# From a weave over two batches to a pipeline over three: linear attention, transposes and attention experts on one Trainium2 core

## The chip, the core and the metric

The kernel runs on one core of a Trainium2 chip. TensorE does matmuls and transposes, VectorE and ScalarE move PSUM to SBUF and do elementwise work, GpSimd does elementwise work on SBUF, and SyncE issues the DMAs. The metric is the device time of one execution in microseconds.

## The reference, cut to what matters

For each of 8 batches a linear attention over 8 heads (576 tokens, 64 dimensions) gives x, and x goes through 4 causal attention experts of which each token uses 2.

```python
kv  = einsum('bhsd,bhse->bhde', k, v)            # linear attention
out = einsum('bhsd,bhde->bhse', q, kv)
x   = out / sqrt(mean(out*out, -1) + 1e-6) * g_norm   # (B, 576, 512)
logits = x @ w_gate                              # top 2 of 4 experts, softmax of the two
for e in range(4):
    q, k, v = x @ wq[e], x @ wk[e], x @ wv[e]    # 512 -> 64
    a = softmax(causal(q @ k.T / 8))
    y += weight[e] * (a @ v @ wo[e])             # where e is one of the token's two
```

## The kernel before

Tokens are handled in five blocks (four of 128 and one of 64). `stage1(b)` is the linear attention of a batch: `p_kv` sums k and v over tokens (L179), `kv_copy` takes it out of PSUM (L187 on VectorE into `kvx`, L188 on ScalarE into `kv2`), `q_block` transposes q (L200), `p_kt` and `p_kg` fold the gate's weights in (L216, L224), and `p_out` (L243) multiplies q by the result. `o_sb` (L250, VectorE), `sq` (L254, ScalarE) and `ms` (L260, VectorE) give the mean squares of a block. Then a chain of small operations on VectorE makes the inverse root by Newton's method: `half` (L271), a first `y` (L273), four passes of `u`, `w`, `y` (L279 to L281). With the last `y`, VectorE makes the gate's logits (L284, L290) and GpSimd the normalized tokens `x_tok`, one tile a block (L296). TensorE transposes these (`p_x`, L307), and ScalarE copies them into `xT`.

`stage2(b)` is the experts: the gate on VectorE (`max`, `sh`, `mk`, `gt`, `gate`, L322 to L341, with an exponential `ex` on ScalarE), the values `p_v` (L347), then for two pairs of experts the projections `p_proj` (L365, cast by ScalarE into `qTp` and `kT`, L376), the scores `p_sc` (L393) with their exponentials into `PT` (ScalarE, L403) and the causal mask (GpSimd, L408), the products `p_O` (L445) with their scaling `osc` (VectorE, L460 to L465), and the transposes `p_OT` (L477). `final(b)` multiplies by `wo` (`p_y`, L501), copies (`y`, L506) and issues the output's DMA; it runs inside the experts of the next batch.

The stages are generators that yield estimated costs. `weave` runs `stage2(b)` and takes pieces of `stage1(b + 1)` so that the latter's `p_out` ends at 72% of the former; the tail of `stage1` (chain, `x_tok`, `p_x`) comes after that. Program order sets priorities; a scheduler may move instructions that are ready. PSUM has two pools: three buffers of two banks ("big": `p_out`, `p_proj`, `p_sc`, `p_O`) and two of one bank ("small": `p_q`, `p_kv`, `p_kt`, `p_kg`, `p_x`, `p_v`, `p_OT`, `p_y`). All DMAs are issued from SyncE's queue in order; the loads of batch b + 2 are issued when step b starts, into one of two sets of buffers.

Of the kernel before, what the change touches and what calls it, by code (L numbers as in the profile page):

```python
# [18 lines left out]
def kernel(  # L19
# [170 lines left out]

    def stage1(b, res):
        qb, kb, vb = loads[b]
# [123 lines left out]

    def stage2(b, res, prev_y):
        xT = res["xT"]
# [25 lines left out]
        for i, (t0, nt) in enumerate(blocks):
            p_v = small([P, E * Hd], "p_v")
            for c in range(NCH):
                nc.tensor.matmul(  # L347
                    p_v[:nt, :],
                    lhsT=xT[:, c, t0 : t0 + nt],
                    rhs=w_r["v"][:, c, :, :].rearrange("p e f -> p (e f)"),  # L350
                    start=(c == 0),
                    stop=(c == NCH - 1),
                )
            nc.vector.tensor_copy(  # L354
                out=vx[:nt, i, :, 0:Hd], in_=p_v[:nt].rearrange("p (e f) -> p e f", e=E)
            )
            yield 0.47

        def proj(pr):
            out_t = []  # L360
            for nm in ("q", "k"):
# [18 lines left out]
                yield 1.0  # L380
            res["qk", pr] = out_t

        def scores(pr):
# [47 lines left out]

        def pv(pr):
            PT = res["PT", pr]
            p_O = big("p_O")
            inv = moe.tile([P, NB, 2], FP32, tag="inv", name="inv")
            osc = moe.tile([P, NB, 2, Hd], BF16, tag="osc", name="osc")
            groups = ((0, (0, 1, 2)), (1, (3, 4)))
            for bank, qcs in groups:
                for n, qc in enumerate(qcs):
                    s0, nq = blocks[qc]  # L440
                    for el in range(2):
                        for kb in range(qc + 1):
# [67 lines left out]

    W1, W2 = 14.0, 14.3
    OUT_END = 11.6 / W1

    def target(a):
        if a < 0.92:
            return min(a / 0.72, 1.0) * OUT_END
        return 1.0

    def weave(main, side):
        a = s = 0.0  # L520
        live = side is not None
        for c in main:
            a += c / W2
            while live and s < target(a):
                try:
                    s += next(side) / W1
                except StopIteration:
                    live = False
        if live:
            for _ in side:  # L530
                pass

    res = {}
    for _ in stage1(0, res):
        pass
# [40 lines left out]
```

## Time and profile before

| | |
|---|---|
| Time, median of 3 runs | 362.43 us (361.71 to 363.38) |
| The profiled execution | 362.53 us, span 360.7 us |
| Mean granted TensorE clock | 0.837 |
| TensorE busy | 291.8 us (81% of the span) |
| VectorE, ScalarE, GpSimd busy | 52%, 42%, 22% |
| HBM traffic | 40.30 MB, mean 112 GB/s |

The profile lists busy time, not useful time: a matmul at granted clock 0.5 (1.2 GHz) is busy longer than one at 1.0 (2.4 GHz). The span runs from the first to the last instruction; the time of an execution also holds what lies around it.

### The profile page before, as it was taken

To read this page: it belongs to the slowest core of one execution; us is meant where nothing else is said; L and a number is where in the kernel's file an instruction comes from. 1 tells how busy PE (TensorE), PEld (TensorE's weight loads), DVE (VectorE), ACT (ScalarE), POOL (GpSimd) and SP (SyncE) were. 2 spreads that over 40 slices of the span, in tenths; PEclk is the share of its full clock that TensorE was granted. 3 is DMA by queue.
4 is the path that set the end of the run, shared out by engine and by line. 5 is a ranking of instruction groups with operands and counts; after the bars stand their busy time and mean duration, and the time that the engine had idled before them with its cause. 6 is when DMAs were issued, how large, how long until landed. Compare 5 with 4: busy or idle time off the path is not lost.

```text
span 360.7 us, 6721 instructions
## 1 busy us (share of the span) xinstructions
PE 291.8 (81%) x2616; PEld 234.8 (65%) x2624; DVE 188.2 (52%) x561; ACT 153.0 (42%) x273; POOL 80.4 (22%) x148
## 2 busy tenths in 40 slices
PE   2782898849994999949995899949996799949883
PEld 2581687638863788638964698638874598728551
DVE  0259654772458444781558444781458534783040
ACT  0202345432581336622572326722663326713833
POOL 8000602150220502150220502141210502132220
PEclk9997599977997599956998599966998589965966
DMA  7968999901737066600872056700002000300213
GB/s 218 214 167 222 241 266 263 207 16 45 220 89 176 2 207 135 185 0 13 250 177 87 2 159 164 195 11 2 2 37 93 2 2 0 133 1 2 88 45 132
DMA packets 75280, 40.30 MB, mean 112 GB/s; under 512 B 54000, under 2 KB 70384, under 8 KB 75248
## 3 DMA queue, kind: packets, MB, share of 16 engines
q1 hardware_dynamic: 75248, 39.86, 42.6%
q8 instruction: 21, 0.34, 0.4%
q14 instruction: 11, 0.09, 0.1%
HBM read 30.42 MB, written 9.44 MB: 110 GB/s over the span
## 4 chain that ended last, share of the span: by engine, by line
PE 56%; issue 22%; ACT 9%; POOL 5%; DVE 4%; DMA 1%; SPq 1%; DVEq 0%; ACTq 0%; POOLq 0%
PE p_proj L365 11%; PE p_x L307 10%; PE p_v L347 7%; PE p_kv L179 7%; PE p_q L200 5%; PE p_out L243 5%; ACT PT L403 4%; POOL x_tok L296 4%; PE p_sc L393 4%; PE p_kg L224 2%; PE p_y L501 2%; DVE o_sb L250 2%; DMA v_b<-in_v_dram 1%; POOL PT L408 1%; ACT y L506 1%
## 5 line engine op out<-in xcount | busy, mean ns | idle before, releaser
L307 PE MATMUL p_x<-ident_f,x_tok 128*128 128x128 f32 (+1 forms) x160 | 39.2, 411 | 39.2 <-POOL x_tok L296 38.1
L408 POOL TENSOR_SCALAR_AFFINE_SELECT PT<-PT 128x256 bf16<-128x256 bf16 (+1 forms) x80 | 29.9, 383 | 167.8 <-ACT PT L403 167.0
L296 POOL TENSOR_TENSOR x_tok<-o_sb,y 128x512 f32<-128x512 f32 (+1 forms) x40 | 42.1, 1083 | 96.7 <-DVE y L281 96.7
L403 ACT ACTIVATE PT<-p_sc 128x576 bf16<-128x576 f32 (+3 forms) x80 | 53.5, 712 | 17.7 <-PE p_sc L393 17.6
L307 PEld LDWEIGHTS p_x<-ident_f,x_tok 128*128 128x128 f32 (+1 forms) x160 | 26.9, 216 | 48.5 <-POOL x_tok L296 45.3
L243 PE MATMUL p_out<-kvx,qT 128*128 128x136 f32 (+1 forms) x320 | 45.8, 291 | 1.6 <-ACT PT L403 0.6
L243 PEld LDWEIGHTS p_out<-kvx,qT 128*128 128x128 f32 (+1 forms) x320 | 38.9, 182 | 6.3 <-ACT PT L403 3.3
L205 DVE COPY qT<-p_q 128x512 f32<-128x512 f32 (+1 forms) x40 | 24.8, 637 | 27.7 <-PE p_q L200 27.7
L354 DVE CAST vext<-p_v 128x256 bf16<-128x256 f32 (+1 forms) x40 | 17.0, 425 | 39.5 <-PE p_v L347 39.1
L254 ACT ACTIVATE sq<-p_out 128x512 f32<-128x512 f32 (+1 forms) x40 | 23.8, 595 | 27.8 <-DVE o_sb L250 19.2
L250 DVE COPY o_sb<-p_out 128x544 f32<-128x544 f32 (+1 forms) x40 | 28.8, 720 | 12.9 <-PE p_out L243 10.6
L260 DVE TENSOR_REDUCE ms<-sq 128x8 f32<-128x520 f32 (+1 forms) x40 | 27.3, 684 | 12.7 <-ACT sq L254 12.7
L445 PE MATMUL p_O<-vext,PT 128*128 128x65 bf16 (+2 forms) x480 | 29.1, 200 | 4.9 <-DVE osc L465 4.2
L179 PE MATMUL p_kv<-v_b,k_b 128*64 128x64 f32 x512 | 28.1, 275 | 6.0 <-DMA v_b<-in_v_dram 5.9
L445 PEld LDWEIGHTS <-PT 128*128 128x128 bf16 (+2 forms) x480 | 23.2, 103 | 13.8 <-issue 9.7
L179 PEld LDWEIGHTS p_kv<-v_b,k_b 128*64 128x64 f32 x512 | 25.2, 187 | 8.0 <-DMA k_b<-in_k_dram 4.5
L347 PE MATMUL p_v<-wv_r,xT 128*128 128x256 f32 (+1 forms) x160 | 30.4, 329 | 0.0
L312 ACT CAST xT<-p_x 128x512 fp32r<-128x512 f32 (+1 forms) x40 | 21.7, 543 | 18.0 <-PE p_x L307 17.9
L393 PE MATMUL p_sc<-qTp,kT 64*128 64x288 f32 (+2 forms) x192 | 25.0, 338 | 2.3 <-ACT PT L403 1.5
L347 PEld LDWEIGHTS p_v<-wv_r,xT 128*128 128x128 f32 (+1 forms) x160 | 25.0, 215 | 1.8
L365 PE MATMUL p_proj<-xT,wq_r 128*128 128x288 f32 x128 | 25.7, 321 | 0.3 <-ACT PT L403 0.3
L501 PE MATMUL p_y<-wo_b,OT 128*128 128x512 bf16 (+1 forms) x72 | 23.4, 409 | 1.8 <-ACT OT L482 1.4
(67 smaller groups left out, 370.5 us busy)
## 6 DMA issues: line engine op xcount, KB each, us to landing
q_b<-in_q_dram SPq DMA_DIRECT2D x32, 256.0 KB, 4.7
out_dram<-y SPq DMA_DIRECT2D x32, 256.0 KB, 2.0
k_b<-in_k_dram SPq DMA_DIRECT2D x7, 1024.0 KB, 5.8
v_b<-in_v_dram SPq DMA_DIRECT2D x7, 1024.0 KB, 8.6
k_b<-in_k_dram SPq DMA_DIRECT2D x4, 256.0 KB, 4.2
v_b<-in_v_dram SPq DMA_DIRECT2D x4, 256.0 KB, 4.5
k_rem<-in_k_dram SPq DMA_DIRECT2D x8, 128.0 KB, 8.5
v_rem<-in_v_dram SPq DMA_DIRECT2D x8, 128.0 KB, 7.5
```

Source lines behind the costliest of these rows:

```text
L179: nc.tensor.matmul(p_kv[hh * Dh : (hh + 1) * Dh, c, :], lhsT=lk, rhs=rv, start=(j == 0), stop=(j == NF), skip_group_check=True,)
L243: nc.tensor.matmul(p_o[:nt, c // 2, (c % 2) * 2 * GW : (c % 2 + 1) * 2 * GW], lhsT=qT[:, c, t0 : t0 + nt], rhs=kvb[:, c, :, :].rearrange(" ...
L250: nc.vector.tensor_copy(out=ob[:nt, i].rearrange("p (k h) g -> p k (h g)", k=2), in_=p_o[:nt, :, 0 : 4 * GW])
L296: nc.gpsimd.tensor_tensor(out=xt[:nt], in0=ob[:nt, i, :, 0:Dh], in1=y[:nt, i * H : (i + 1) * H].unsqueeze(2).to_broadcast([nt, H, Dh]), op ...
L307: nc.tensor.transpose(p_x[:, c, :nt], xts[i][:nt, 2 * c : 2 * c + 2, :].rearrange("p h d -> p (h d)"), ident_f[:nt, :nt],)
L347: nc.tensor.matmul(p_v[:nt, :], lhsT=xT[:, c, t0 : t0 + nt], rhs=w_r["v"][:, c, :, :].rearrange("p e f -> p (e f)"), start=(c == 0), stop= ...
L365: nc.tensor.matmul(p_p[:, s, 0:HALF], lhsT=w_r[nm][:, c, 2 * pr : 2 * pr + 2, :].rearrange("p e f -> p (e f)"), rhs=xT[:, c, s * HALF : (s ...
L393: nc.tensor.matmul(p_s[:, el, o : o + hi - lo], lhsT=kTp[pb, kb * P : (kb + 1) * P], rhs=qTp[pb, lo:hi], start=True, stop=True,)
L403: nc.scalar.activation(PT[:, :, d0 : d0 + o], p_s[:, :, 0:o], ACTF.Exp, scale=scale)
L408: nc.gpsimd.affine_select(out=d, in_=d, compare_op=AluOpType.is_ge, fill=0.0, base=0, pattern=[[0, 2], [1, w]], channel_multiplier=-1,)
L445: nc.tensor.matmul(p_O[:nq, bank, (2 * n + el) * (Hd + 1) : (2 * n + el + 1) * (Hd + 1)], lhsT=PT[:nk, el, col : col + nq], rhs=vx[:nk, kb ...
L501: nc.tensor.matmul(p_y[:nq, :], lhsT=OT[:, pr, s0 : s0 + nq], rhs=wo_b[:, pr, :], start=(pr == 0), stop=(pr == EP - 1),)
```

## The change

`stage1` is split. `stage_a(b)` holds the linear attention up to `x_tok`, now with three Newton passes instead of four (and the factor subtracted the other way round, `reverse0=True`, so that no sign alternates). `stage_x(b)` holds the transposes `p_x` and the copies into `xT`. `stage2` becomes `stage_s`: `p_v` is a generator of its own, and a string of keys sets the order in which the pieces of one batch's experts are taken. `merge` takes pieces from up to three streams, each spread over a given part of the step: the experts of b over all of it, the transposes of b + 1 from 0.05 to 0.4, the linear attention of b + 2 from 0.1 on. A prologue does the attention of batch 0, and then the transposes of batch 0 and the attention of batch 1 side by side. Loads are issued one batch further ahead (b + 3 when step b starts).

```diff
-    def stage1(b, res):
+    def stage_a(b, res):
...
-        for it in range(4):
+        for it in range(3):
...
             xts.append(xt)
-        yield 0.0
+        res["x_tok"] = xts
+
+
+    def stage_x(res):
+        xts = res["x_tok"]
+        xT = s1.tile([P, NCH, S], FP32R, tag="xT", name="xT")
         for i, (t0, nt) in enumerate(blocks):
             p_x = small([P, NCH, P], "p_x")
...
-    def stage2(b, res, prev_y):
+    def stage_s(b, res, prev_y):
...
-        yield from proj(0)
-        yield from scores(0)
-        yield from proj(1)
-        yield from scores(1)
-        if prev_y is not None:
-            yield from prev_y
-        yield from pv(0)
-        yield from o_t(0)
-        yield from pv(1)
-        yield from o_t(1)
-        res["OT"] = OT
-
+        st = {"V": v_proj(), "Q0": proj(0), "Q1": proj(1), "S0": scores(0), "S1": scores(1)}
+        st.update({"P0": pv(0), "P1": pv(1), "T0": o_t(0), "T1": o_t(1), "Y": prev_y})
+        order = (
+            "Q0 Q0 V V S0 V S0 V S0 V S0 Q1 S0 Q1 S1 Y S1 Y S1 P0 P0 P0 S1 P0 P0 S1 Y T0 Y Y P1 P1 P1 P1 P1 T1"
+        )
+        for key in order.split():
+            if st[key] is not None:
+                yield next(st[key])
...
+    def merge(*streams):
+        live = [[t0, t0, (t1 - t0) / cost, gen] for gen, cost, t0, t1 in streams if gen is not None]
+        while live:
+            x = min(live, key=lambda x: x[0])
+            try:
+                x[0] += next(x[3]) * x[2]
+            except StopIteration:
+                live.remove(x)
+
+    CA, CX, CS = 11.8, 2.25, 14.5
+    res = [dict() for _ in range(B)]
+    merge((stage_a(0, res[0]), CA, 0.0, 1.0))
+    loads[2] = load_qkv(2)
+    merge((stage_x(res[0]), CX, 0.3, 0.6), (stage_a(1, res[1]), CA, 0.0, 1.0))
     y_gen = None
     for b in range(B):
-        if b + 2 < B:
-            loads[b + 2] = load_qkv(b + 2)
-        nxt = {}
-        weave(stage2(b, res, y_gen), stage1(b + 1, nxt) if b + 1 < B else None)
-        y_gen = final(b, res["OT"])
-        res = nxt
+        if b + 3 < B:
+            loads[b + 3] = load_qkv(b + 3)
+        merge(
+            (stage_s(b, res[b], y_gen), CS, 0.0, 1.0),
+            (stage_x(res[b + 1]) if b + 1 < B else None, CX, 0.05, 0.4),
+            (stage_a(b + 2, res[b + 2]) if b + 2 < B else None, CA, 0.1, 1.0),
+        )
+        y_gen = final(b, res[b]["OT"])
```

How this moves instructions, at two places. First TensorE's queue at the seam of two steps (line, operation, out<-in, shape, count). Before, `p_x` follows directly on the last `p_OT` of the experts:

```order
L477 MATMUL p_OT<-ident_b,osc 128x64
L307 MATMUL p_x<-ident_f,x_tok 128x128 x12
...
L307 MATMUL p_x<-ident_f,x_tok 128x128 x4
L365 MATMUL p_proj<-xT,wq_r 128x288
L307 MATMUL p_x<-ident_f,x_tok 128x64 x4
L365 MATMUL p_proj<-xT,wk_r 128x288
L347 MATMUL p_v<-wv_r,xT 128x256 x4
L179 MATMUL p_kv<-v_b,k_b 64x64 x8
```

Now the last `p_out` of batch b + 2 is followed by the projections of the next step, the rest of `p_O` and `p_OT` (18 and 5, left out here but for one each), and its first scores; `p_x` of batch b + 2 comes after these, one block before `p_kv` of the batch after it:

```order
L242 MATMUL p_out<-kvx_110,qT 64x136 x4
L373 MATMUL p_proj<-xT,wq_r 128x288 x8
L373 MATMUL p_proj<-xT,wk_r 128x288 x3
...
L451 MATMUL p_O<-vext_116,PT 128x65
...
L484 MATMUL p_OT<-ident_b,osc 128x128
L373 MATMUL p_proj<-xT,wk_r 128x288 x5
...
L400 MATMUL p_sc<-qTp,kT_134 128x320 x2
L313 MATMUL p_x<-ident_f,x_tok 128x128 x4
L179 MATMUL p_kv<-v_b,k_b 64x64 x8
```

Between the last `p_out` and `p_x` there are now 16 projections and 8 score matmuls that stood behind `p_x` before.

Second VectorE's queue at the same seam. Before, the last `ms` stands behind `osc` of both groups of `p_O`, and the copy of `p_v` (`vext`) is the first thing after `gate`:

```order
L465 TENSOR_TENSOR osc<-p_O,inv 128x384
L465 TENSOR_TENSOR osc<-p_O,inv 128x128
L460 RECIPROCAL inv<-p_O 64x2
L260 TENSOR_REDUCE ms_118<-sq_124 64x8
...
L341 TENSOR_TENSOR gate<-gt,rden 128x20
L354 CAST vext_116<-p_v 128x4x64
L187 COPY kvx_96<-p_kv 64x4x64
```

Now the last `ms` stands ahead of the second group's `osc`, and behind `gate` come both copies of `p_kv`, then those of `p_v`:

```order
L472 TENSOR_TENSOR osc<-p_O,inv 128x384
L259 TENSOR_REDUCE ms_104<-sq_124 64x8
L270 TENSOR_SCALAR half<-ms_104 128x40
...
L472 TENSOR_TENSOR osc<-p_O,inv 128x128
...
L347 TENSOR_TENSOR gate<-gt,rden 128x20
L187 COPY kvx_110<-p_kv 64x4x64 x2
L362 CAST vext_116<-p_v 128x4x64 x4
```

`ms` of the last block moved past one group of `osc`, and `p_kv`'s copies past `p_v`'s.

## Rows read from the trace of the kernel before

**Rows 1.** The page: busy us, share of the span and count, by engine.

```profile
PE 291.8 (81%) x2616; PEld 234.8 (65%) x2624; DVE 188.2 (52%) x561; ACT 153.0 (42%) x273; POOL 80.4 (22%) x148
```

**Rows 2.** Chain that ended last, in time order: start us, us, what.

```profile
198.65 1.19 POOL x_tok L296
```

**Rows 3.** TensorE in order of time: start us, us, line, tiles, count, [idle before].

```profile
199.88 3.15 PE L307 MATMUL p_x<-ident_f,x_tok 128*128 128x128 f32 x12 [4.31 <-POOL x_tok L296]
...
207.06 1.12 PE L179 MATMUL p_kv<-v_b,k_b 128*64 128x64 f32 x16
...
209.23 0.63 PE L179 MATMUL p_kv<-v_b,k_b 128*64 128x64 f32 x16
...
230.98 1.14 PE L243 MATMUL p_out<-kvx,qT 128*64 128x136 f32 x8
...
240.88 3.15 PE L307 MATMUL p_x<-ident_f,x_tok 128*128 128x128 f32 x12 [4.30 <-POOL x_tok L296]
```

**Rows 4.** Windows of one period: length, busy by engine (count), clock share, DMA.

```profile
195.60:199.90 4.30, 0.02 (x1) 0.02 (x1) 3.90 (x24) 0.64 (x1) 1.25 (x2) 0.50 0.00 0
199.90:209.20 9.30, 9.12 (x71) 7.57 (x73) 3.11 (x7) 3.48 (x7) 3.96 (x4) 0.50 0.01 2
209.20:234.00 24.80, 24.55 (x242) 19.93 (x240) 13.67 (x28) 14.78 (x26) 3.73 (x10) 1.00 0.69 186
234.00:236.60 2.60, 1.48 (x21) 1.01 (x19) 2.19 (x13) 0.00 (x0) 0.00 (x0) 0.98 0.23 53
```

**Rows 5.** VectorE in order of time, at the seam of two steps.

```profile
195.24 0.17 DVE L271 TENSOR_SCALAR half<-ms 128x40 int32<-128x40 int32 x1
...
198.37 0.20 DVE L281 SCALAR_TENSOR_TENSOR y<-w,y 128x40 f32<-128x40 f32 x1
...
199.91 0.96 DVE L329 TENSOR_TENSOR sh<-lg,m 128x20 f32<-128x20 f32 x1
200.79 0.17 DVE L333 TENSOR_TENSOR mk<-lg,m 128x20 f32<-128x20 f32 x1
...
202.37 0.53 DVE L341 TENSOR_TENSOR gate<-gt,rden 128x20 f32<-128x20 f32 x1
```

**Rows 6.** TensorE in order of time: head and last start of the transposes.

```profile
12.24 0.46 PE L179 MATMUL p_kv<-v_rem,k_rem 128*64 128x64 f32 x4
...
23.38 5.76 PE L243 MATMUL p_out<-kvx,qT 128*128 128x136 f32 x40
37.09 3.15 PE L307 MATMUL p_x<-ident_f,x_tok 128*128 128x128 f32 x12 [7.96 <-POOL x_tok L296]
...
322.83 3.15 PE L307 MATMUL p_x<-ident_f,x_tok 128*128 128x128 f32 x12 [4.31 <-POOL x_tok L296]
```

**Rows 7.** Issues of the SP queue in order of time, head.

```profile
34.08 0.64 SPq L122 DMA_DIRECT2D v_rem<-in_v_dram  x1
```

**Rows 8.** The page: DMA issues, count, KB each, median us to landing.

```profile
v_rem<-in_v_dram SPq DMA_DIRECT2D x8, 128.0 KB, 7.5
```

**Rows 9.** Windows of the tail.

```profile
329.00:332.00 3.00, 3.00 (x15) 3.00 (x15) 0.85 (x2) 0.11 (x1) 0.00 (x0) 0.50 0.03 5
345.80:353.00 7.20, 5.62 (x48) 3.76 (x49) 2.81 (x15) 1.28 (x2) 0.05 (x1) 0.50 0.09 20
353.00:360.70 7.70, 3.43 (x8) 0.81 (x7) 0.00 (x0) 2.92 (x5) 0.00 (x0) 0.72 0.44 154
```

**Rows 10.** TensorE in order of time: two prices at the full clock.

```profile
191.04 1.72 PE L445 MATMUL p_O<-vext,PT 128*128 128x65 bf16 x30
...
218.47 1.33 PE L365 MATMUL p_proj<-xT,wq_r 128*128 128x288 f32 x8
```

**Rows 11.** Groups by line: busy us, mean ns of one | idle before.

```profile
L376 ACT CAST kT<-p_proj 128x576 fp32r<-128x576 f32 x16 | 10.2, 639 | 19.0 <-PE p_proj L365 19.0
...
L187 DVE COPY kvx<-p_kv 64x256 f32<-64x256 f32 x16 | 6.7, 422 | 34.3 <-PE p_kv L179 33.9 <-ACT kv L188 0.2
...
L188 ACT COPY kv<-p_kv 64x256 f32<-64x256 f32 x16 | 5.9, 367 | 40.7 <-DVE kvx L187 40.6
```

More of the change, by code (lines that the diff above doesn't have):

```diff
@@ L280, in stage1 @@
             nc.vector.tensor_tensor(out=w[:], in0=u[:], in1=m, op=AluOpType.mult)
-            nc.vector.scalar_tensor_tensor(out=y2[:], in0=w[:], scalar=1.5, in1=y[:], op0=AluOpType.subtract, op1=AluOpType.mult)
+            nc.vector.scalar_tensor_tensor(
+                out=y2[:], in0=w[:], scalar=1.5, in1=y[:], op0=AluOpType.subtract, op1=AluOpType.mult, reverse0=True
+            )
             y = y2
@@ L343, in stage2, with v_proj @@
         vx = vexts[b % 2]
[L344 to L352, printed above, removed]
-                )
[L354 to L357, printed above, removed]
+        def v_proj():
+            for i, (t0, nt) in enumerate(blocks):
+                p_v = small([P, E * Hd], "p_v")
+                for c in range(NCH):
+                    nc.tensor.matmul(
+                        p_v[:nt, :],
+                        lhsT=xT[:, c, t0 : t0 + nt],
+                        rhs=w_r["v"][:, c, :, :].rearrange("p e f -> p (e f)"),
+                        start=(c == 0),
+                        stop=(c == NCH - 1),
+                    )
+                nc.vector.tensor_copy(
+                    out=vx[:nt, i, :, 0:Hd], in_=p_v[:nt].rearrange("p (e f) -> p e f", e=E)
+                )
+                yield 0.47
         def proj(pr):
-            out_t = []
+            out_t = res["qk", pr] = []
             for nm in ("q", "k"):
@@ L380, in proj @@
                 yield 1.0
-            res["qk", pr] = out_t
         def scores(pr):
             qTp, kTp = res["qk", pr]
-            PT = moe.tile([P, 2, strips], BF16, tag="PT", name="PT", bufs=3)
+            PT = res["PT", pr] = moe.tile([P, 2, strips], BF16, tag="PT", name="PT", bufs=3)
             def piece(parts):
@@ L427, in scores @@
             yield 0.2
-            res["PT", pr] = PT
-        OT = moe.tile([P, EP, S], BF16, tag="OT", name="OT")
+        OT = res["OT"] = moe.tile([P, EP, S], BF16, tag="OT", name="OT")
         def pv(pr):
@@ L435, in pv @@
             inv = moe.tile([P, NB, 2], FP32, tag="inv", name="inv")
-            osc = moe.tile([P, NB, 2, Hd], BF16, tag="osc", name="osc")
+            osc = res["osc", pr] = moe.tile([P, NB, 2, Hd], BF16, tag="osc", name="osc")
             groups = ((0, (0, 1, 2)), (1, (3, 4)))
@@ L451, in pv @@
                             )
-                    yield 0.11 * (qc + 1)
+                    if qc != qcs[-1]:
+                        yield 0.11 * (qc + 1)
                 for sub in ((qcs,) if bank == 0 else ((3,), (4,))):
@@ L470, in pv @@
                     )
-            res["osc", pr] = osc
+                yield 0.11 * (qcs[-1] + 1)
         def o_t(pr):
@@ L508, in final @@
             yield 0.45
[L511 to L535, printed above, removed]
+    def merge(*streams):
[11 more added lines that the diff above has]
+    merge((stage_x(res[0]), CX, 0.3, 0.6), (stage_a(1, res[1]), CA, 0.0, 1.0))
     y_gen = None
     for b in range(B):
-        if b + 2 < B:
-            loads[b + 2] = load_qkv(b + 2)
-        nxt = {}
-        weave(stage2(b, res, y_gen), stage1(b + 1, nxt) if b + 1 < B else None)
-        y_gen = final(b, res["OT"])
-        res = nxt
+        if b + 3 < B:
[4 more added lines that the diff above has]
+            (stage_a(b + 2, res[b + 2]) if b + 2 < B else None, CA, 0.1, 1.0),
+        )
+        y_gen = final(b, res[b]["OT"])
     for _ in y_gen:
```

4 lines of the change are left out of this document (3 added, 1 removed).

## The prediction

> **What bounds the kernel now.** I read the page first, then the chain that ended last, then one period engine by engine, then its windows. The page says TensorE is busy 81% of the span, with every other engine near half or below [rows 1]; that alone would leave little to win. The chain says where the rest goes: in every batch it leaves TensorE for GpSimd's `x_tok` and comes back at the transposes `p_x` [rows 2]. The starts of `p_x` give the frame: batch 0 at 37.09, batch 7 at 322.83 [rows 6], so the span is a head of 37.09, seven periods of 285.74 / 7 = 40.8 us, and a tail of 360.70 - 322.83 = 37.87. I price one late period, 199.88 to 240.88 = 41.0 us [rows 3].
>
> Its windows [rows 4] show three losses. First, 4.3 us in which TensorE does nothing while VectorE walks from `half` (195.24) to the last `y` (198.37) and GpSimd makes the first `x_tok` tile [rows 5]. Second, 9.30 us afterwards in which it is busy 9.12 us at granted clock 0.50, which is 1.2 GHz; sixteen `p_kv` matmuls take 1.12 us there and 0.63 us once the clock is back at 2.4 GHz [rows 3], so I count half of the 9.12, 4.56 us, as lost, and 0.18 us idle. Third, 2.60 us before the gap with only 1.48 busy. What is left is the work at the full clock: 24.8 + 1.48 + 4.56 = **30.8 us a period**; 41.0 - 30.8 = 10.2 us is what a cover for the seam can give back.
>
> **The change, part by part.** The matmuls are the same, so a full step (experts of b, transposes of b+1, attention of b+2) still holds 30.8 us of TensorE work. New is what TensorE has in its queue between the last `p_out` of one batch and that batch's first `p_x`. Before, that path is 232.12 (end of the last `p_out`) to 240.88 = 8.76 us [rows 3], with only the rest of `p_O` and `p_OT` to fill it. Now 16 projections of the next step, 18 `p_O`, 5 `p_OT` and 8 score matmuls stand there. A projection costs 1.33 / 8 = 0.17 us or a little less back to back (0.15), a `p_O` 1.72 / 30 = 0.057 [rows 10]; with scores (288 columns and more) at a projection's price and 0.1 for a `p_OT`, this is 2.4 + 1.0 + 0.5 + 1.2 = 5.1 us of cover.
>
> Waits that I expect at the new seam, per step:
> - *The first scores wait for the cast of `kT`.* They now follow the last `wk_r` projection with two `p_OT` between; the cast takes 0.64 us on ScalarE [rows 11]. Wait 0.6.
> - *The second group of `p_O`* waits for `osc` of the first (VectorE does `osc` behind `o_sb`): 0.4, between 0 (hidden by the projections) and 1.
> - *The first `p_x`.* The path of 8.76 loses one Newton pass, three operations: from `half` to the start of the last `y`, thirteen operations on, the chain takes 3.13 us, 0.24 a piece [rows 5], so 0.7. It also loses about 1.2, since `ms` of the last block now stands ahead of the second group's `osc`, not behind it. That is 6.9 against 5.1 + 0.6 + 0.4 = 6.1 of cover and waits: 0.8 left, between 0 and 2.0 (if the reordering gives nothing).
> - *The first `p_v`* needs the PSUM buffer of `p_kv`. Its copies now stand on VectorE behind `sh` ... `gate`; before, TensorE was waiting at that time anyway. `gate` ends at 202.90, 3.0 us after `p_x` began [rows 3, 5], or 4.0 if `ex` stands behind an exponential on ScalarE; then two `kvx` and two `kv2` copies in turn, 2 x (0.42 + 0.37) = 1.6 [rows 11]: 4.6 to 5.6 after `p_x` starts. TensorE gets there after `p_x` 0.4, `p_kv` 2.3 (80 matmuls at about 0.63 for 16, overlapping, 0.029 each), `p_x` 0.4, six projections 0.9: 4.0. Wait 0.6 to 1.6, I take 1.1.
>
> Together 2.9 us, so a step is 30.8 + 2.9 = **33.7 us**, bounds 31.4 (only the two surest waits, halved) and 37.5 (their upper ends and 3 us of small waits in the denser middle, where `p_x` and `p_v` alternate on two PSUM buffers).
>
> Do the waits bring the clock down? The trace has both cases: 24.8 us with waits well below a microsecond stay at 1.00, but the gap's window is at 0.50 from its start, after a stretch with 1.48 us busy in 2.60 [rows 4], and in the tail 7.2 us stay at 0.50 with TensorE busy 5.62 of them [rows 9]. So broken work can cost the clock, not only the long gap. The new seam is busy about 9 us in 12, more than either stretch, and I take it as staying at 2.4 GHz. The Trainium skill (TensorE: Matmul & The Clock Gate, section "A second HAM failure mode: psum-queue depth-cycling") speaks against this: short waits between groups of matmuls, from cycling PSUM buffers, make the clock swing between its levels, and the price is paid again at each burst. By that rule a step would be 2.3 to 4.6 us longer; the tail's window agrees with the rule, the 24.8 us at 1.00 do not.
>
> Other edits: splitting off `v_proj`, `stage_x` and the order string only set the order. The loads of b+3 are issued a step ahead as those of b+2 were; the middle window moves 186 GB/s at 0.69 of the DMA engines [rows 4] and a step needs no more bytes than before, in 33.7 us where it had 41.0. I cost them at nothing; if a load came late it would show as a `p_kv` wait on DMA, a few us in the first step or two.
>
> **The sum.** *Head.* `p_x` of batch 0 starts 0.7 earlier, at 36.4, but now attention of batch 1 runs beside it. Its last keys hang on `v_rem`, issued at 34.08 [rows 7], landing about 7.5 us later [rows 8]: 41.6, `p_kv` done near 43. From there to the last `p_out` batch 0 took 29.14 - 12.70 = 16.4 us [rows 6], at low-clock prices and with first-use waits; half of it is 8.2, and I take 10 since the clock comes back only on the way: 53.0, bounds 51 and 59. *Six full steps* (b = 0 to 5): 6 x 33.7 = 202.2. *Steps 6 and 7* hold no attention. The tail of before does one batch's experts from 329.0 to 353.0 = 24.0, of which 3.0 / 2 + 5.62 / 2 = 4.3 is lost to the low clock [rows 9]: 19.7 at best. Step 6 also has `p_x` (2.1): 23; step 7 21.5; together 44.5, bounds 39.4 and 50. *Last outputs* 7.7 as now [rows 9]. Sum 53.0 + 202.2 + 44.5 + 7.7 = 307.4. The profiled execution of before took 362.53 for a span of 360.70; with those 1.83 us, **309.2 us**. That execution is 0.1 above the median of 362.43, so no correction.
>
> **The rivals.**
> 1. *The clock falls at every seam.* For it: the tail's window; against it: the denser cover. Half to all of the 4.56 us lost now, six times: 14 to 28 more, 323 to 337, about 330.
> 2. *VectorE's queue holds TensorE longer.* Every PSUM copy stands in one queue with the chain and `gate`; if the copies of `p_kv`, `p_v` and `p_q` come 2 us later in each step than worked out, 309 + 12 = 321. For it: VectorE has 3.90 us busy of 4.3 in the gap [rows 4]; against it: TensorE's sequence puts projections in front.
> 3. *The waits hide.* TensorE's other work absorbs them and the two last steps run at 39.4: 51 + 6 x 31.4 + 39.4 + 7.7 + 1.8 = 288 with all at once; half of that way, 298.
> 4. *Slower than before.* The finer mix of score, `p_O`, transpose and output matmuls never holds the full clock: each us of TensorE work done at 1.2 GHz costs half a us. The gain of 53 us is 8.9 a step, so it decides from 17.7 us of each step at the low clock (now 9.3). Wholly at the low clock, a step is 61 us and the kernel some 470. The 24.8 us at 1.00 on much the same mix speak against it.
> 5. *The change doesn't do what it says*: `p_x` is placed too early and TensorE still waits the full path, 8.8 less 5.1 = 3.7 a step where I took 0.8 (with 1.0 more after it): 309 + 17 = 326, most of it inside rival 1's range.
>
> **How the numbers follow.** Forecast, 302 to 317: 54%. Rival 1: 20%; rival 2: 7%; rival 5: 5%; rival 3: 11%; rival 4: 3%. A chance of 8 in 10 is the forecast with most of rivals 1, 2 and 5 and the near half of rival 3: 297 to 331. Half a per cent, 1.8 us, is about what a measurement can tell from no change (the three runs spread 1.7). Faster by more than that 0.96, same 0.01, slower 0.03.
>
> **What would show it.** Starts of `p_x` about 33.7 us apart in steps 1 to 5; idle time of TensorE before `p_x` of about 1 us a step instead of 4.3; clock 1.00 through whole steps; the wait of `p_v` on the copies of `p_kv` about 1 us; the last `p_out` of batch 1 near 53. I am wrong if the clock falls in each step (rival 1), if the waits on VectorE pass 4 us a step (2, 5), or if the head ends after 59 because batch 1's loads come late.

## The result, and the profile after

The changed kernel takes 324.18 us (median of 4 runs, 323.54 to 328.55), the kernel before 362.07 beside it (4 runs, 360.21 to 363.38): a ratio of 0.895, 95% interval 0.890 to 0.900. The ratios are taken over runs within 1.5% of their kernel's fastest, the medians over all, and of the profiled executions below, those of two passes and of the square from SBUF are slow ones. The forecast of 309.2 was 15 us too low, in its direction right, and 324 lies in the range of 297 to 331. The profiled execution took 324.47 us for a span of 322.5, so what has to be explained is 322.5 against the sum of 307.4.

From the page of the changed kernel, the rows that answer to [rows 1] and the granted clock in 40 slices:

```profile
PE 276.0 (86%) x2624; PEld 220.4 (68%) x2624; DVE 189.2 (59%) x537; ACT 153.0 (47%) x273; POOL 79.5 (25%) x148
...
PEclk9959599999999999799999999799999999899977
```

TensorE does the same matmuls in 276.0 us, not 291.8, and less of them run at 1.2 GHz: the mean granted clock is 0.945, not 0.837, and the clock row is full but for the head, the tail and three dips. From the views of waits (who waits for whom, us in all, times, longest), first the kernel before, then the changed one:

```profile
PE p_x L307 <- POOL x_tok L296: 38.1, 9, 8.0
```

```profile
PE p_kv L179 <- DMA v_b<-in_v_dram: 10.3, 5, 4.5
PE p_sc L400 <- ACT PT L410: 5.9, 9, 0.9
PE p_sc L400 <- ACT kT L384: 4.7, 7, 0.7
PE p_x L313 <- POOL x_tok L297: 4.3, 3, 2.5
...
PE p_proj L373 <- ACT qTp L384: 3.6, 5, 0.7
```

The transposes' waits on GpSimd are nearly gone; what is left of them falls in the first 95 us, and the waits of `p_kv` on its loads in the first 33.

Two late seams and what follows each, in windows that answer to [rows 4] (length, then busy us of PE, PEld, DVE, ACT, POOL with counts, granted clock, DMA share, GB/s):

```profile
193.90:201.90 8.00, 5.38 (x48) 4.12 (x48) 6.59 (x31) 3.75 (x8) 1.24 (x2) 1.00 0.22 51
201.90:206.00 4.10, 4.10 (x72) 3.77 (x74) 2.64 (x6) 2.11 (x5) 4.10 (x5) 0.58 0.00 0
206.00:230.60 24.60, 24.56 (x217) 19.79 (x213) 13.88 (x31) 12.94 (x24) 3.45 (x10) 1.00 0.14 49
230.60:238.60 8.00, 5.41 (x48) 4.13 (x48) 6.57 (x32) 3.75 (x8) 1.27 (x2) 1.00 0.00 1
238.60:242.00 3.40, 3.40 (x87) 3.17 (x88) 2.36 (x5) 1.98 (x4) 3.40 (x4) 1.00 0.02 5
242.00:266.10 24.10, 23.77 (x196) 19.00 (x194) 14.39 (x32) 13.00 (x24) 4.13 (x11) 1.00 0.14 50
```

A seam, from the end of the last `p_out` to the first `p_x`, is 8.0 us with 5.4 of TensorE work in it, each time. Behind the first of these two the clock is at 0.58 for 4 us, behind the second it stays at 1.00. The same holds for the others: it dips behind 129.7 (0.64 for 4.8 us), 201.9 and 274.2 (0.62 for 3.8 us), not behind 166.4 and 238.6.

The second of these seams on TensorE in order of time (start us, us, what, and in brackets the wait before it and what ended it; answers to [rows 3]):

```profile
229.42 1.14 PE L242 MATMUL p_out<-kvx,qT 128*64 128x136 f32 x8
230.88 1.33 PE L373 MATMUL p_proj<-xT,wq_r 128*128 128x288 f32 x8 [0.32 <-ACT sq L253]
232.94 0.67 PE L373 MATMUL p_proj<-xT,wk_r 128*128 128x288 f32 x3 [0.73 <-ACT qTp L384]
233.46 1.19 PE L451 MATMUL p_O<-vext,PT 128*128 128x65 bf16 x18
...
236.37 0.40 PE L400 MATMUL p_sc<-qTp,kT 64*128 64x288 f32 x2 [0.66 <-ACT kT L384]
...
238.09 0.41 PE L400 MATMUL p_sc<-qTp,kT 64*128 64x320 f32 x2 [0.86 <-ACT PT L410]
238.56 0.66 PE L313 MATMUL p_x<-ident_f,x_tok 128*128 128x128 f32 x4
...
244.58 0.74 PE L355 MATMUL p_v<-wv_r,xT 128*128 128x256 f32 x4 [0.33 <-ACT kv L188]
```

Here `p_x` waits for nothing, and four waits on ScalarE stand ahead of it. GpSimd's row shows that this reading deceives: it began two `x_tok` tiles at 237.33 and took 2.18 us for both, so the first was there at about 238.4, and `p_x` started at 238.56. Hidden waits or not, the chain through `y` is just in time.

```profile
234.13 0.18 DVE L270 TENSOR_SCALAR half<-ms 128x40 int32<-128x40 int32 x1
...
235.09 0.29 DVE L472 TENSOR_TENSOR osc<-p_O,inv 128x128 bf16<-128x128 f32 x1
...
237.05 0.20 DVE L280 SCALAR_TENSOR_TENSOR y<-w,y 128x40 f32<-128x40 f32 x1
237.33 2.18 POOL L297 TENSOR_TENSOR x_tok<-o_sb,y 128x512 f32<-128x512 f32 x2 [11.74 <-DVE y L280]
```

The last `y` ends 6.69 us behind the last `p_out`, and GpSimd starts 0.08 us after it; in the other late seams it is the same to 0.03 us.

**Where the 15 us are.** The last `p_out` of batches 1 to 7 ends at 55.54, 88.28, 121.70, 158.37, 193.88, 230.56 and 266.11 (start and length of its last row added, as 229.42 + 1.14), and the last outputs start at 314.29. So the head is 55.5 (forecast 53.0), the six steps 210.6 (202.2), steps 6 and 7 48.2 (44.5), the last outputs 8.2 (7.7): 2.5 + 8.4 + 3.7 + 0.5 = 15.1. The six steps are 32.74, 33.42, 36.67, 35.51, 36.68 and 35.55 long; the first holds no `p_y`, and the late ones alternate with the clock.

### The profile page after: what moved, and what is told of

Its sections match the earlier page's. It is cut to its first block, busy times and chain, and to the rows that moved or that the text cites. A ratio compares the mean times of both kernels' runs of the same rounds, so it can differ in the third digit from the quotient of the medians.

```text
span 322.5 us, 6704 instructions
## 1 busy us (share of the span) xinstructions
PE 276.0 (86%) x2624; PEld 220.4 (68%) x2624; DVE 189.2 (59%) x537; ACT 153.0 (47%) x273; POOL 79.5 (25%) x148
## 4 chain that ended last, share of the span: by engine, by line
PE 70%; DVE 10%; ACT 9%; SPq 4%; issue 3%; POOL 1%; DMA 1%; DVEq 0%; ACTq 0%; POOLq 0%
PE p_proj L373 11%; PE p_out L242 11%; PE p_v L355 7%; PE p_sc L400 7%; PE p_O L451 7%; PE p_y L506 6%; PE p_q L200 6%; PE p_x L313 6%; PE p_kv L179 5%; ACT PT L410 3%; PE p_kg L224 3%; DVE o_sb L249 3%; SPq L134 2%; PE p_OT L484 2%; POOL x_tok L297 1%
## 5 line engine op out<-in xcount | busy, mean ns | idle before, releaser
L415 POOL TENSOR_SCALAR_AFFINE_SELECT PT<-PT 128x256 bf16<-128x256 bf16 (+1 forms) x80 | 29.3, 381 | 143.4 <-ACT PT L410 143.4
L242 PE MATMUL p_out<-kvx,qT 128*128 128x136 f32 (+1 forms) x320 | 48.1, 292 | 0.0
L400 PE MATMUL p_sc<-qTp,kT 64*128 64x288 f32 (+2 forms) x192 | 35.7, 358 | 10.7 <-ACT PT L410 5.9
L318 ACT CAST xT<-p_x 128x512 fp32r<-128x512 f32 (+1 forms) x40 | 21.8, 545 | 34.3 <-PE p_x L313 34.3
L400 PEld LDWEIGHTS p_sc<-qTp,kT 64*128 64x128 f32 x192 | 19.8, 185 | 21.9 <-ACT PT L410 8.5
L179 PE MATMUL p_kv<-v_b,k_b 128*64 128x64 f32 x512 | 25.7, 260 | 10.3 <-DMA v_b<-in_v_dram 10.3
L179 PEld LDWEIGHTS p_kv<-v_b,k_b 128*64 128x64 f32 x512 | 23.0, 173 | 12.2 <-DMA k_b<-in_k_dram 6.7
L313 PE MATMUL p_x<-ident_f,x_tok 128*128 128x128 f32 (+1 forms) x160 | 25.9, 289 | 5.4 <-POOL x_tok L297 4.3
L355 PE MATMUL p_v<-wv_r,xT 128*128 128x256 f32 (+1 forms) x160 | 28.3, 300 | 0.7 <-ACT kv L188 0.7
L373 PE MATMUL p_proj<-xT,wk_r 128*128 128x288 f32 x128 | 24.3, 314 | 3.6 <-ACT qTp L384 3.6
L506 PE MATMUL p_y<-wo_b,OT 128*128 128x512 bf16 (+1 forms) x80 | 25.1, 417 | 0.7 <-ACT OT L489 0.7
L511 ACT COPY y<-p_y 128x512 f32<-128x512 f32 (+1 forms) x40 | 23.0, 595 | 5.0 <-PE p_y L506 2.7
```

The costliest lines, as they stand in the source:

```text
L179: nc.tensor.matmul(p_kv[hh * Dh : (hh + 1) * Dh, c, :], lhsT=lk, rhs=rv, start=(j == 0), stop=(j == NF), skip_group_check=True,)
L242: nc.tensor.matmul(p_o[:nt, c // 2, (c % 2) * 2 * GW : (c % 2 + 1) * 2 * GW], lhsT=qT[:, c, t0 : t0 + nt], rhs=kvb[:, c, :, :].rearrange(" ...
L313: nc.tensor.transpose(p_x[:, c, :nt], xts[i][:nt, 2 * c : 2 * c + 2, :].rearrange("p h d -> p (h d)"), ident_f[:nt, :nt],)
L355: nc.tensor.matmul(p_v[:nt, :], lhsT=xT[:, c, t0 : t0 + nt], rhs=w_r["v"][:, c, :, :].rearrange("p e f -> p (e f)"), start=(c == 0), stop= ...
L373: nc.tensor.matmul(p_p[:, s, 0:HALF], lhsT=w_r[nm][:, c, 2 * pr : 2 * pr + 2, :].rearrange("p e f -> p (e f)"), rhs=xT[:, c, s * HALF : (s ...
L400: nc.tensor.matmul(p_s[:, el, o : o + hi - lo], lhsT=kTp[pb, kb * P : (kb + 1) * P], rhs=qTp[pb, lo:hi], start=True, stop=True,)
```

## The experiments

Steps are taken from last `p_out` to last `p_out` of a late step, idle is the sum of the waits that TensorE's rows show in it, and work is the rest. The totals of these kernels scatter by several us with the head, whose first steps depend on when loads land, so the steps are compared first. Late steps of all kernels:

| kernel | seam, us | idle, us | work, us | step, us |
|---|---|---|---|---|
| before | 8.77 | 5.6 | 35.4 | 41.0 |
| before, three passes | 8.06 | 5.1 and 4.8 | 33.0 and 35.5 | 38.07 and 40.3 |
| one pass | 6.58 | 1.7 | 32.7 | 34.4 |
| two passes | 7.30 | 2.3 | 32.1 | 34.45 |
| the change (three passes) | 8.00 | 2.9 and 2.6 | 32.6 and 34.1 | 35.5 and 36.7 |
| four passes | 9.07 | 2.9 | 34.5 | 37.4 |
| square from SBUF | 8.23 | 2.7 | 34.1 and 35.1 | 36.8 and 37.7 |
| `p_kv` first | 7.55 | 0.7 | 33.6 | 34.3 |

**How long the chain is: one and four Newton passes.** These kernels leave out two passes, or add one, so `y` has another exactness.

```diff
-        for it in range(3):
+        for it in range(1):      # the other kernel: range(4)
```

> The changed kernel with one Newton pass (leaves out two passes, so x is normalized only roughly; the time alone is read). My theory: the waits left at the seam are on PSUM buffers and casts of ScalarE, not on the chain, so 1.4 us less of chain brings 0 to -4 us (the wait of p_v on the copies of p_kv, 0.33 a step, goes). Rival 'the chain still sets the seam': -1.4 in each of 7 seams, about -10 us, span near 312.

> The changed kernel with four Newton passes again (undoes that part alone). My theory: in the late steps the first p_x starts at the moment its x_tok is there (no wait left, but no slack either), so a chain 0.7 us longer gives a wait of about 0.6 us on x_tok in each of 7 seams: about +4.5 us, span near 327. Rival 'the seam has slack': 0, span 322 to 323. Rival 'the chain bounds the seam with all that hangs on it, VectorE's copies too': +0.7 to 1.4 a seam, span 328 to 332.

One pass: 318.51 us (314.46 to 318.92), ratio 0.880, interval 0.872 to 0.888, span 312.6. Four passes: 332.12 us (331.69 to 333.94), ratio 0.922, interval 0.914 to 0.930, span 329.8. By the totals the one pass alone wouldn't decide: the median is 5.7 us less than the change's, between my 0 to 4 and the rival's 10, and the profiled execution is the fastest of the four. The seams decide. They follow the chain, 6.58, 8.00 and 9.07 us, so my view that the shorter chain would give little, since `p_x` shows no wait, fell, and the rival held; the span with four passes lies in the range of its second rival. TensorE with one pass:

```profile
230.17 0.40 PE L400 MATMUL p_sc<-qTp,kT 64*128 64x288 f32 x2 [0.66 <-ACT kT L384]
230.41 0.20 PE L484 MATMUL p_OT<-ident_b,osc 64*128 64x64 bf16 x1
230.45 0.37 PE L400 MATMUL p_sc<-qTp,kT 64*128 64x288 f32 x1
230.96 0.66 PE L313 MATMUL p_x<-ident_f,x_tok 128*128 128x128 f32 x4
```

Three scores stand ahead of `p_x` here, eight in the change. The likeliest reading, which no run tests by itself, is that the scheduler that writes TensorE's queue puts `p_x` where it reckons `x_tok` to be ready, and fills the time until then with scores, which wait for ScalarE. So a chain that is too long shows as waits of the scores, not of `p_x`. With four passes even the eight scores don't fill it, `p_x` waits 0.34 us, and the rows behind it run at the low clock (GpSimd's rows and TensorE's):

```profile
243.44 0.47 POOL L415 TENSOR_SCALAR_AFFINE_SELECT PT<-PT 128x256 bf16<-128x256 bf16 x1 [12.50 <-ACT PT L410]
243.88 5.07 POOL L297 TENSOR_TENSOR x_tok<-o_sb,y 128x512 f32<-128x512 f32 x5
244.97 1.12 PE L313 MATMUL p_x<-ident_f,x_tok 128*128 128x128 f32 x4 [0.34 <-POOL x_tok L297]
246.02 1.12 PE L179 MATMUL p_kv<-v_b,k_b 128*64 128x64 f32 x16
```

The fourth pass lengthens the seam by 1.07 us, not by its own 0.7, because GpSimd makes a causal mask (L415) between the last `y` and the first `x_tok`, which starts 0.60 us after that `y` instead of 0.08. It does so in each late seam with four passes, and in none with one, two or three.

**The same with two passes.** The edit is `range(2)`.

> The changed kernel with two Newton passes, not three (y is less exact by the pass left out). Theory (the chain sets the seam): 0.7 us less per seam, seven seams, and some of the low clock behind them gone: span 315 to 318. Rival (the seam's waits are ScalarE's own, since p_x hardly waits by the profile): span 321 to 323.

The late seams are 7.30 us and the steps 34.45, so the chain sets the seam, 0.7 us a pass, as the theory has it. The middle of the 4 runs, 322.90 us (317.56 to 323.65), doesn't show it; the fastest run does. In the profiled execution (span 321.0, the rival's number) the last `p_out` of batch 1 ends at 60.31 where the change has 55.54; from there on it takes 260.7 us, the change 267.0. By steps, a pass costs nothing from one to two (34.4, 34.45), as the work shrinks by what the waits grow. From two to three it costs 1.1 us at the full clock (35.5), half of it work, and 1.15 more where the clock falls behind the seam (36.7). From three to four it costs 0.7 between steps with such a dip (37.4), and the dip comes behind four of five late seams instead of three. Why the work moves at the full clock isn't shown.

**Three passes in the kernel before.** Only this part of the change:

```diff
-        for it in range(4):
+        for it in range(3):
...
-                out=y2[:], in0=w[:], scalar=1.5, in1=y[:], op0=AluOpType.subtract, op1=AluOpType.mult)
+                out=y2[:], in0=w[:], scalar=1.5, in1=y[:], op0=AluOpType.subtract, op1=AluOpType.mult, reverse0=True)
```

> The kernel before with three Newton passes, not four, and the last operation of each pass with its operands swapped as in the change: only this part of the change. Theory (the chain is wholly on the path there): 0.7 us in each of eight batches, 5.6 us, span 354 to 356. Rival (part of it hidden by the rest of p_O and p_OT): under 2 us, span 359 to 361.

348.73 us (348.44 to 350.52), ratio 0.966, interval 0.961 to 0.970, span 348.6: 12.6 us come off the kernel before beside it (361.31), twice what the chain's 0.7 in eight batches gives, so the theory had the direction but not the size. Two of its seams in windows, the gap and what follows:

```profile
149.80:153.40 3.60, 0.02 (x1) 0.02 (x1) 3.29 (x21) 0.64 (x1) 1.24 (x2) 0.50 0.00 0
153.40:162.60 9.20, 8.80 (x117) 7.50 (x118) 2.98 (x9) 3.58 (x8) 3.97 (x4) 0.83 0.01 2
...
187.90:191.40 3.50, 0.00 (x0) 0.00 (x0) 3.23 (x20) 0.64 (x1) 1.18 (x2) 0.50 0.00 0
191.40:200.70 9.30, 9.07 (x69) 7.52 (x71) 2.54 (x8) 3.48 (x7) 4.03 (x4) 0.50 0.01 2
```

The gap is 3.58 us instead of 4.3, and in some periods the clock comes back inside the stretch behind it (0.83 against 0.50 before, [rows 4]): such a period is 38.07 us, the others 40.3. So what a shortened gap gives back is its own length and, in some periods, 2.2 us of clock. A third of the change's 38 us is in this edit alone.

**Without the pipeline over three batches.** The order inside a step and the three passes stay; the transposes of b+1 go back behind the step, and attention and loads run one batch less ahead.

```diff
-    loads[2] = load_qkv(2)
-    merge((stage_x(res[0]), CX, 0.3, 0.6), (stage_a(1, res[1]), CA, 0.0, 1.0))
+    merge((stage_x(res[0]), CX, 0.0, 1.0))
...
-        if b + 3 < B:
-            loads[b + 3] = load_qkv(b + 3)
+        if b + 2 < B:
+            loads[b + 2] = load_qkv(b + 2)
...
-            (stage_x(res[b + 1]) if b + 1 < B else None, CX, 0.05, 0.4),
-            (stage_a(b + 2, res[b + 2]) if b + 2 < B else None, CA, 0.1, 1.0),
+            (stage_a(b + 1, res[b + 1]) if b + 1 < B else None, CA, 0.0, 0.95),
         )
+        if b + 1 < B:
+            merge((stage_x(res[b + 1]), CX, 0.0, 1.0))
```

> The changed kernel with the pipeline taken back to two batches: in step b the attention of b+1 runs beside the experts of b, then the transposes of b+1, then the next step; order string, generators, three passes stay. My theory (the gain is the cover that other batches' work gives the chain): the idle time before p_x and the low clock behind it come back, about 40 us a step, span 345 to 360. Rival 'the finer order of the experts and the three passes give the gain': span 320 to 335.

360.47 us (358.51 to 361.02), ratio 0.997, interval 0.993 to 1.000, span 358.7: no gain that can be told from none, as the theory had it. Its late steps are 40.5 to 42.3 us; `p_x` waits again, and behind each seam comes a stretch with a lower clock, 0.57 to 0.82 over 9.7 us. The waits of the whole run and one such stretch:

```profile
PE p_x L313 <- POOL x_tok L297: 26.3, 9, 7.2
```

```profile
202.30:212.00 9.70, 9.68 (x114) 7.90 (x115) 2.50 (x8) 3.60 (x8) 4.00 (x4) 0.76 0.01 2
```

It doesn't keep the 12 us that the shorter chain gave above. Against a step of 38.07 us there, a step of 40.8 here has 0.7 us more waits and 2.1 more work: its 20 `p_x`, which all run at the low clock, take 4.70 us, not 3.72, and the scores 3.67, not 2.85. Why the scores are dearer isn't settled. The pipeline itself is what covers the seam.

**A `p_out` buffer that is free sooner.** The square reads `o_sb` in SBUF, not `p_out` in PSUM:

```diff
-                p_o[:nt, :, 0 : 4 * GW].rearrange("p k (h g) -> p k h g", g=GW)[:, :, :, 0:Dh],
+                ob[:nt, i].rearrange("p (k h) g -> p k h g", k=2)[:, :, :, 0:Dh],
```

> The changed kernel with sq computed from o_sb in SBUF instead of from p_out in PSUM, so that p_out's buffer is free after VectorE's copy alone. My theory: the seam's first projection waits 0.32 us for sq, and p_out's loads wait for it in the middle: -0.3 to -0.6 us a step, -2 to -4 us in all, and no PE wait on ACT sq in the trace. Rival 'ScalarE's other work holds the buffers': 0. A cost is possible if ScalarE reads SBUF slower than PSUM (0.60 us a piece now).

335.64 us (332.18 to 338.39), ratio 0.927, interval 0.918 to 0.936: each run is slower than each of the change's, and my expectation fell. The first projection no longer waits and the scores wait less, but the seam doesn't get shorter (8.23 us): the wait stands in one piece in front of `p_x`, and the clock falls behind all five late seams (0.50 to 0.66 for the next 4 us). One of these seams on VectorE, TensorE and GpSimd, in order of time:

```profile
246.23 0.20 DVE L280 SCALAR_TENSOR_TENSOR y<-w,y 128x40 f32<-128x40 f32 x1
246.48 0.49 PE L400 MATMUL p_sc<-qTp,kT 64*128 64x320 f32 x2 [0.34 <-ACT PT L410]
246.50 0.56 POOL L415 TENSOR_SCALAR_AFFINE_SELECT PT<-PT 128x256 bf16<-128x256 bf16 x1 [11.51 <-ACT PT L410]
247.03 3.07 POOL L297 TENSOR_TENSOR x_tok<-o_sb,y 128x512 f32<-128x512 f32 x3
248.12 1.11 PE L313 MATMUL p_x<-ident_f,x_tok 128*128 128x128 f32 x4 [1.14 <-POOL x_tok L297]
```

The chain on VectorE is even 0.16 us shorter: the last `y` ends 6.53 us behind the last `p_out` (239.90), in the change 6.69. What takes this back and more is GpSimd: as with four passes, it makes a causal mask first, and `x_tok` starts 0.60 us after the last `y`, in all five late seams. So the wait on the square did not set the seam; `x_tok` did. What the edit would give with the mask behind `x_tok` isn't shown.

**Work that needs nothing of the seam, put into it.** The attention of b+2 starts with 80 `p_kv`, 2.5 us:

```diff
-            (stage_a(b + 2, res[b + 2]) if b + 2 < B else None, CA, 0.1, 1.0),
+            (stage_a(b + 2, res[b + 2]) if b + 2 < B else None, CA, 0.0, 1.0),
```

> The changed kernel with one number other: the attention of batch b+2 starts at 0.0 of a step, not at 0.1, so that its 80 p_kv matmuls (2.5 us, which need nothing of this seam) stand on TensorE ahead of the first p_x and of the first scores. Theory (the normalization chain sets the seam: 8.0 us from the end of the last p_out to the first p_x, with 5.4 us of TensorE work in it): the seam stays near 8 us, its work grows to 7.9, its idle time falls from 2.6 to under 0.5, and the low clock behind it goes; a step gets some 2.3 us shorter, the span 302 to 308, the time 304 to 310. Rival 1 (VectorE's queue): the four copies of p_kv, 1.6 us, now stand in that chain, the seam grows to 9 to 9.6 us with a wait of p_x on x_tok of about 1.5, and the span is 314 to 318. Rival 2 (the waits are ScalarE's, for the casts of qTp and kT and the first exponential): they stay as they are, span 320 to 324.

> Both edits at once: attention of b+2 from 0.0 and two Newton passes. If p_kv fills the seam, the chain has nothing more to give: within 2 us of the kernel with the first edit alone. If p_x still waits there for the chain, 0.7 us a seam comes off: about 5 us less than with the first edit alone.

319.81 us (317.24 to 324.02), ratio 0.882, interval 0.875 to 0.889, span 315.2; with two passes as well 319.30 us (318.38 to 320.31), ratio 0.883, interval 0.880 to 0.887. Seam and body of a late step of the first:

```profile
192.50:200.10 7.60, 6.86 (x121) 6.11 (x120) 6.73 (x32) 3.11 (x5) 1.62 (x2) 1.00 0.09 22
200.10:226.90 26.80, 26.45 (x211) 20.01 (x209) 15.72 (x37) 16.25 (x29) 7.30 (x14) 1.00 0.13 45
```

The seam is full, one wait of 0.7 is left in the step, the clock is 1.00 from 97 us to the last outputs, and the chain no longer matters: a pass less changes nothing (34.3 and 34.3). That is the mechanism as the theory had it, though the span of 315.2 lies in the range of the first rival, whose signs (a longer seam, a wait of `p_x`) are not there. Two things close the seam together: in this order the last `y` also comes sooner, 5.84 us behind the last `p_out` and not 6.69, since ScalarE makes the last `sq` ahead of the cast of `qTp` and not behind it. How much each gives isn't separated. The size was not as the theory had it. A step gains 1.8 us (36.1 to 34.3) where I expected 2.3 plus the clock, because the work rose from 32.6 to 33.6: the rows of `p_O`, `p_q`, `p_kv` and the scores each take some tenths more in this order (`p_kv` 2.88 against 2.48). In the first seam `p_kv` is cut in two by other work and the rows behind run at the low clock, 1.07 us for sixteen `p_kv` instead of 0.64, so that the last `p_out` of batch 2 ends 1.3 us later than in the change (89.58). It computes what the change computes, and none of the kernels here that do so can be told to be faster.

**The head.** First the loads of batch 1 ahead of those of `wq` and `wk`, which wait for the one staging buffer with everything behind them in SyncE's queue; then this with `p_kv` first, and with the square from SBUF too; last the weights' loads on GpSimd's queue (the last two lines) and `wo` behind batch 2, with `p_kv` first.

```diff
         w_r[name] = wr
+        if name == "v":
+            loads[1] = load_qkv(1)
-    loads[1] = load_qkv(1)
...
-            nc.sync.dma_start(wf[:, :, e, :], wdram[e].rearrange("(c p) f -> p c f", p=P))
+            nc.gpsimd.dma_start(wf[:, :, e, :], wdram[e].rearrange("(c p) f -> p c f", p=P))
```

> The changed kernel with the loads of batch 1 issued right behind those of the weight wv, ahead of wq and wk, whose loads wait for the one staging buffer and hold the queue behind them (in the changed kernel v_b of batch 1 is issued at 26.81 and k_rem at 33.25). Theory (the head is late because these loads are issued late): the last p_out of batch 1 ends at 50 to 52, not at 55.5, and the span is 317 to 320. Rival (the head hangs on the bandwidth, since the transfers run at their full share to 72 us, or on the chain of batch 0): the last p_out of batch 1 stays within 1 us of 55.5, or the next step gives it back; span 321 to 324.

> Attention of b+2 from 0.0 of a step, and the loads of batch 1 ahead of wq and wk. If the head hangs on the issue of the loads: 3 to 5 us less than with the first edit alone (span 315.2), so 310 to 312. If it hangs on bandwidth, the p_kv of batch 2, which stand earlier here, wait for their loads instead: 314 to 317.

> The same with the square taken from o_sb, not from PSUM, so that a p_out buffer is free when o_sb is written. Theory (with p_kv in the seam the chain no longer bounds it; what is left is the wait of the first projection for that buffer, 0.7 us a step): 0.7 x 6 = 4 us less than without it, a step of 33.6 us. Rival (the chain is still near the bound; this edit made its seam 0.2 us longer and moved the seam's waits to p_x, with the low clock in more seams): no gain, or up to 8 us more.

> Attention of b+2 from 0.0 of a step, the loads of wq, wk and wv issued from GpSimd's queue, and wo loaded behind batch 2, so that no load that waits for the one staging buffer stands ahead of a batch's loads in SyncE's queue. Theory (the head is late because that queue is held: moving the loads of batch 1 alone only moved the hold to v_b of batch 2): last p_out of batch 1 by 50 to 53 and a first step of 33 to 35 behind it, the last p_out of batch 2 at 84 to 87 (89.6 with the first edit alone), later steps 34.3 as before; span 309 to 313. Rival (bandwidth: three batches and the weights are 12 MB whatever their order): last p_out of batch 2 at 88.5 to 91, span 314 to 318; or GpSimd, held by the weights' loads, makes the first x_tok late, and the head is longer than before.

None gained. *Batch 1 early* on the change: 327.32 us (326.67 to 328.98). The last `p_out` of batch 1 ends 1.8 us sooner, at 53.76, but the first step behind it takes 36.9 us instead of 32.7, so the rival held: the next step gives it back. Now `wk` is late. Its loads wait for the staging buffer until 51.27, VectorE casts them at 56.92, TensorE's projections wait 2.69 us, and the clock is 0.50 to 0.56 from 58 to 65 us. That `v_b` of batch 2 is held too costs nothing that shows: no `p_kv` of that step waits for a load. SyncE's queue, VectorE and TensorE there:

```profile
35.08 0.60 SPq L116 DMA_DIRECT2D k_b<-in_k_dram  x1
51.27 2.02 SPq L158 DMA_DIRECT2D w_stage<-in_moe_wk_dram  x4
53.33 0.51 SPq L116 DMA_DIRECT2D v_b<-in_v_dram  x1
56.92 0.73 DVE L159 TENSOR_SCALAR wk_r<-w_stage,g_wide 128x1024 fp32r<-128x1024 f32 x1
57.80 1.68 PE L374 MATMUL p_proj<-xT,wk_r 128*128 128x288 f32 x8 [2.69 <-DVE half L271]
```

*With `p_kv` first* 318.46 us (317.42 to 321.36), *and the square from SBUF* 318.04 (316.85 to 322.26): neither differs from `p_kv` first alone by what these runs can tell. In the last the wait of 0.7 is gone from the late steps, but they stay at 34.3, with work at 33.8; so my theory that this wait was the next bound fell. *Weights on GpSimd's queue*: 324.97 us (324.21 to 327.7), ratio 0.902, interval 0.897 to 0.907. The second rival held in what it foresaw, a late first `x_tok` and a longer head, but through VectorE, not GpSimd. In the change four loads of 128 KB for `wq` land in 2.6 us (median); here they run from another queue beside a batch's loads and take 8.4:

```profile
w_stage<-in_moe_wq_dram POOLq DMA_DIRECT2D x4, 128.0 KB, 8.4
```

VectorE waits 4.3 and 4.6 us for them and those of `wk`, with the first chain behind in its queue, and the first `x_tok` starts at 48.87, so the last `p_out` of batch 2 ends at 100.19 (89.58 with `p_kv` first alone). The late steps are 34.3 again.

## Why the prediction was right, and where it was 15 us off

- *The seam and its cover: right in kind.* A step waits 2.9 us, as I summed, but not where I put it. I let the chain's path shrink from 8.76 by 0.7 for the pass and 1.2 for `ms` that now stands ahead of `osc`; it is 8.00, and the kernel before with three passes has 8.06, so on balance only the pass counted. Of the 1.2, 0.55 is there: `half` starts 3.57 us behind the last `p_out`, not 4.12. But the second group's `osc` now stands between the chain's operations on VectorE, which take 3.1 us from `half` to the end of the last `y`, in the kernel before with three passes 2.6. The wait of the first scores on the cast of `kT` is 0.66 (forecast 0.6); the rest is 0.32 on the square, 0.73 on a cast and 0.86 on an exponential in the place of 0.4 for `osc` and `p_x`'s own 0.8, and `p_v` waits 0.33, not 1.1.
- *The work of a step: the term that failed.* I took 30.8 us, by counting half of the 9.12 at low clock as lost and the rest as unchanged. The change's undisturbed late step has 32.6. Tile by tile (from each row's start to the next, less the waits shown), the tiles that lay in the low stretch give back 3.2 of 35.4, not 4.6 (`p_x` 4.29 to 2.46, `p_kv` 3.43 to 2.48, `p_proj`, `p_v` and `p_kt` together 0.4), and the others cost 0.4 more (scores with `p_OT` +0.65, `p_out` +0.34, `p_y` and `p_O` -0.6). In four late steps that is 4 x 1.8 = 7.2 us. Why scores and `p_out` are dearer in the finer mix isn't settled; `p_kv` first, with a mix finer still, has 33.6.
- *The clock: rival 1 came half true.* It fell behind three of the five late seams, two of them in the six steps. The price shows between two steps in the same order with the same waits in the seam: 36.7 against 35.5, so 1.15 us each (1.5 more work, less the wait of `p_v`, 0.33, which is gone then), where I had 2.3 to 4.6. 7.2 + 2.3, less 1.2 for the two first steps that came out shorter than 33.7, is the 8.4 of the six steps to 0.1. I had taken the clock as staying up because the seam's cover, about 9 us in 12, is denser than the stretches at 0.50; but 5.62 in 7.20 [rows 9] is denser than that, so the comparison spoke for nothing. The Trainium skill's rule that I weighed (TensorE: Matmul & The Clock Gate, section "A second HAM failure mode: psum-queue depth-cycling"), short waits between groups of matmuls that bring the clock down again and again, agrees with these dips, and with four in five late seams at four passes, but not with the seams at 1.00 that have the same waits.
- *Head, +2.5.* `p_kv` of batch 1 ends at 42.3, near the 43 that I had; from there to the last `p_out` it takes 13.2 us where I put 10. Of these, 2.3 are waits, the longest that of `p_kt` on the copy of `p_kv`, 1.64.
- *Steps 6 and 7, +3.7.* They open with a seam of 8.0 us and a dip of the clock. `p_kv` first, with a seam of 7.35, 1.4 us of idle time in it and no dip, takes 45.8 from the same point to the last outputs, so some 2.4 of the 3.7 hang on these; that is an estimate between two orders.
- *The range.* 324.2 lies outside my forecast's 302 to 317 and in the 323 to 337 of rival 1, but only 2.3 us of the six steps' 8.4 are the clock's. The range of 297 to 331 held because it takes in most of the rivals, and the term that missed most, the work, is the reason of none of them: in that it held by luck. The upper bound of 37.5 for a step isn't the sum of its terms either: 30.8, the upper ends of the four waits (5.2) and 3 are 39.0. No step reached either.
- *The other rivals.* VectorE's queue (2), as I meant it, was not the cause: no wait of TensorE on a copy by VectorE shows in a late step. But the chain that sets the seam runs in that queue, which is busy 6.6 of the 8.0 us. Rival 5, `p_x` placed too early, is nearer than `p_x`'s zero wait makes it look: the seam's idle time is 2.6 us, where I had 1.8 and the rival 3.7. The kernel is not slower (4), and the undone pipeline shows that the gain is the cover.

## What to carry to other kernels

When a scheduler writes the queues, a chain that is too long hides: the engine's waits get the names of whatever was put in front, and removing those waits doesn't close the gap (the square from SBUF) while shortening the chain or putting independent work into the seam closes it (one pass, `p_kv` first). Follow the chain through every engine that it crosses: a mask of 0.5 us that GpSimd made ahead of `x_tok` shows on TensorE as a wait for `x_tok` alone. Price a seam by its length from the last to the first dependent instruction, less the work in it, and the work by steps that ran at the full clock, not by halving a slow stretch. And stop there: steps of 34.3 to 34.5 us came out of seven kernels here, with idle times from 0.4 to 2.3 us, so where the clock doesn't dip, neither chain nor buffers nor waits gave anything more here. What holds them there isn't shown.

## What the runs showed of the hardware that was not expected

The granted clock can fall in one step and not in the next, with the same order and the same waits: seams of 8.0 us with 2.6 of idle time, cut into pieces of 0.3 to 0.9, are followed by 0.64, 1.00, 0.58, 1.00 and 0.62. With four passes it fell behind four of five late seams (0.60 to 0.66 for the next 4.2 us), with two behind one of five, with one behind none. Which of it the chip looks at, these rows don't show. And loads of 128 KB that landed in 2.6 us from SyncE's queue took 8.4 from GpSimd's, beside a batch's loads. The trace lists the two queues as different kinds (hardware_dynamic and software_dynamic), so whether the company or the kind of queue makes the difference, these runs don't show.
